# A second half that takes key and query groups in turn, the contraction behind them with every denominator, and row and key sums on VectorE

## The chip, the cores and the metric

One core of a Trainium2 chip runs the kernel. The metric is the device time of one launch in microseconds (us). The kernel before has a median of 2421.54 us over three runs (2417.6 to 2421.97).

## What is computed

The reference, cut to what matters (S = 2048 tokens, D = 1024, 32 heads of 32, F = 3584, all float32):

```python
xn = _layernorm(x)                      # (x - mean) / sqrt(var + 1e-5)
q, k, v = split(xn @ wqkv)              # 32 heads
phi = lambda t: where(t > 0, t + 1, exp(t)) + 1e-6
kv  = einsum("bhsd,bhse->bhde", phi(k), v)
z   = einsum("bhsd->bhd", phi(k))
num = einsum("bhqd,bhde->bhqe", phi(q), kv)
den = einsum("bhqd,bhd->bhq", phi(q), z)[..., None] + 1e-6
s   = (num / den) @ wo
h   = silu(xn @ w1) * (xn @ w3)         # the GLU is fed with xn too
out = x + s * silu(h @ w2)
```

## The kernel before, in words

**Arithmetic.** Each float32 operand is split into a high and a low part (ScalarE casts, line L93; VectorE subtracts, L94), and each product is three matmuls (L101, L102, L103). A 2x2 blocked product is made with seven block products instead of eight (`gemm`), so every operand also needs sums of its blocks: T1, T2, T3, T4 of the weights (VectorE, L342), S1 to S4 of the normalised rows.

**A gemm.** It uses four PSUM banks in the order a, b, c, d, a, c, d. VectorE adds the bank b to u (L453), c to make c22 (L460), d onto c22 (L466), then c21 (L481) and c12 (L489). The second product into bank c may start only when the add of L460 has read it. Behind each product the gemm takes one step of the next weight group (`next(stages)`) and one slot of `catch_up`: it runs the first entry of the list `later`, and if that is empty one step of the first generator in `jobs`. A gemm has six slots. Engines run in program order, so what a slot puts on VectorE stands between the gemm's own adds.

**Two halves of 1024 tokens** (`half(h)`): four key gemms (a pair of 128-column blocks each), four query gemms, then fourteen pairs of a gate and an up gemm. In the second half the key gemms are followed by the contraction (`row_products`): rows of x and of the keys are read back from DRAM and multiplied over all tokens, giving g_d, from which kv is made later (`key_values`, L902). Key gemms 0 and 1 of the second half run side by side.

**Keys.** phi is a relu (L495) and an exp (L496) on ScalarE and one VectorE operation (L497). The result pk is then turned by TensorE (`to_rows`, L503, into a bank trk) and copied by ScalarE (L504) to y; this turn is an entry of `later`. A fifth entry, `sums`, makes three sums on GpSimd (L538 to L540). GpSimd issues the stores to y_d (L507).

**Jobs in the slots.** In the first half: four `prepare_next` (normalise and turn 128-row blocks of the second half; four sums of row blocks on GpSimd, L259, L260, L267, L268), then 28 `weight_sums` of w2 (GpSimd, L755 to L758). In the second half: eight `denominators` jobs during the contraction (`first_denominators`); then, in the slots of the query and gate/up gemms, `key_values` and `merge_wo`, the divides of the first half's tokens, the other eight denominator jobs and eight more divides. A divide waits four slots when m < LATE, loads a tile qd through SyncE (L865) and works on VectorE (L873 and four sums). What is left of the jobs at the end of the half is run at once (`for j, _ in jobs: run(j)`). Tiles of jobs share four buffers (tag "job").

**GpSimd** also makes sums of the gated rows throughout (hs, L719 to L723), on 128x256 tiles. SyncE issues most loads in program order, so a load whose buffer is not free holds those behind it.

Of the kernel before, what the change touches and what calls it, by code (L numbers as in the profile page):

```python
# [16 lines left out]
P = 128  # L17
# [5 lines left out]
def tile_linear_attention_times_swiglu(  # L23
# [29 lines left out]

    ident = const.tile([P, P], F32, name="ident")
    make_identity(nc, ident)
    hmask = const.tile([P, P], F32, name="hmask")
    nc.vector.memset(hmask, 0.0)
    for i in range(P // DH):
# [55 lines left out]
    def small(name):  # L114
        return pc.tile([P, C], F32, tag="c", name=name)
# [105 lines left out]
    def prepare_next(i):  # L221


        def turn(n, src):
            p_ = bank(f"t{n}1_{i}")
            for k in range(ND // 2):
                nc.tensor.transpose(p_[:, k * P:(k + 1) * P], src[:, k * P:(k + 1) * P], ident)
            return p_

        def steps(_):  # L230
            t = [job_tile([P, D], f"xn{i}_{e}") for e in range(2)]
            for c in range(2):
# [24 lines left out]
            keep_rows(1, i, "A22", a22)  # L257
            g = job_tile([P, 2, C], f"xg{i}")
            nc.gpsimd.tensor_add(out=g[:, 0], in0=a21, in1=a22)  # L259
            nc.gpsimd.tensor_sub(out=g[:, 1], in0=a11, in1=a21)  # L260
# [6 lines left out]
            nc.gpsimd.tensor_sub(out=g[:, 0], in0=g[:, 0], in1=a11)  # L267
            nc.gpsimd.tensor_sub(out=g[:, 1], in0=a12, in1=g[:, 0])  # L268
            yield True
            keep_rows(1, i, "S2", g.rearrange("p n c -> p (n c)"))  # L270
            p_ = turn("A11", a11)
            keep("A11", p_)
            nc.scalar.copy(out=a11, in_=p_)
            yield True
            p_ = turn("A12", a12)
            keep("A12", p_)
            nc.scalar.copy(out=a12, in_=p_)
            yield True
            p_ = turn("A22", a22)
# [216 lines left out]
        nc.scalar.activation(dst, dst, AF.Exp, scale=-1.0)  # L496
        nc.vector.scalar_tensor_tensor(dst, src, 0.0, dst, op0=ALU.max, op1=ALU.add, accum_out=z)  # L497

    def to_rows(dst, src, name, bias=0.0):

        p_ = bank(f"tr{name}")
        for t in range(C // P):
            nc.tensor.transpose(p_[:, t * P:(t + 1) * P], src[:, t * P:(t + 1) * P], ident)  # L503
        nc.scalar.activation(dst, p_.rearrange("p (t d) -> p t d", t=C // P), AF.Identity, bias=bias)  # L504

    def keep_keys(h, pair, n, t):
        nc.gpsimd.dma_start(out=y_d[h][:, :, YS.index(n), pair], in_=t.rearrange("p (t d) -> p t d", d=P))  # L507

    def key_rows(h, pair):

        rows, pairs = {}, {}

        def use(n, c, src):
            j = 2 * pair + n
# [5 lines left out]
            later.append(lambda: turn(n, c, pk))  # L520

        def turn(n, c, pk):
            if (c, n) == (0, 0):
                t = rows[c, n] = small(f"y00_{h}_{pair}")
            else:
                if (1 - c, 1) not in pairs:
                    pairs[1 - c, 1] = job_tile([P, 2, C], f"y{c}_{h}_{pair}")
                t = rows[c, n] = pairs[1 - c, 1][:, n if c else 0]
            to_rows(t.rearrange("p (t d) -> p t d", d=P), pk, f"k{h}_{pair}_{n}{c}", 1e-6)
            if (c, n) != (1, 1):  # L530
                keep_keys(h, pair, f"Y{c}{n}", t)
            if len(rows) == 4:
                later.append(sums)

        def sums():
            y01, y10, y11 = rows[0, 1], rows[1, 0], rows[1, 1]
            r4, r2 = pairs[1, 1][:, 1], small(f"r2_{h}_{pair}")
            nc.gpsimd.tensor_add(out=r4, in0=y01, in1=y11)  # L538
            nc.gpsimd.tensor_sub(out=y11, in0=y11, in1=y10)
            nc.gpsimd.tensor_add(out=r2, in0=y11, in1=y01)  # L540
            for n, t in (("R4", r4), ("R5", y11), ("R2", r2)):
                keep_keys(h, pair, n, t)

        return use

    def row_products():
# [39 lines left out]
        for at, s in enumerate(steps):  # L586
# [3 lines left out]
            if at + 1 < len(steps):  # L590
                split_[steps[at + 1]] = ready(*steps[at + 1])
            if at + 2 == len(steps):
                ops["q1_0_"].ask()
# [49 lines left out]
    def half(h):  # L643
# [9 lines left out]
        def side_by_side(*gemms):  # L653
            for _ in zip_longest(*gemms):
                pass

        uses = [key_rows(h, pair) for pair in range(ND // 2)]
        if h == 0:
            mom = st.tile([P, TH, 2], F32, tag="mom", bufs=1, name="mom")
# [21 lines left out]
        if h == 0:  # L681
            for g in m:
                run(g)
        else:
            side_by_side(keys(0, paired=True), keys(1, paired=True))
            for pair in range(2, ND // 2):
                run(keys(pair))
            jobs.append((first_denominators(), False))
            for _ in row_products():
                pass  # L690
        jobs.append((attention_work(), False) if h else (next_work(), True))
        for pair in range(ND // 2):

            def use_q(n, c, src):
                j = 2 * pair + n
                pq = signed(f"pq{h}_{j}_{c}")
                phi(src, pq)
                nc.gpsimd.dma_start(out=pq_d[j // JG][2 * h + c][:, j % JG], in_=pq)  # L698
# [126 lines left out]
    def denominators(c):  # L825
# [29 lines left out]
    def divide(m, k):  # L855
# [12 lines left out]
            return t  # L868

        def steps(t):  # L870
            for _ in range(4 if m < LATE else 3):
                yield True
            nc.vector.scalar_tensor_tensor(t[:, :2], t[:, :2], 1e-6, t[:, 2:], op0=ALU.add, op1=ALU.mult)  # L873
            for _ in four_sums(t[:, 0], t[:, 1], t[:, 2], t[:, 3], nc.vector):
# [11 lines left out]
    def key_values(j):  # L886
# [87 lines left out]
    for h in range(NH):  # L974
        some = [Operands(wqkv, part * D + pair * 2 * P, f"{'qk'[part]}{h}_{pair}_", h == 0 and part == 1,
                         h and part == 1 and pair == 1)
                for part in (1, 0) for pair in range(ND // 2)]
# [6 lines left out]
    for o, o.next in zip(ops, ops[1:]):  # L984
        pass
    ops = {o.name: o for o in ops}
    after_rows = [ops["q1_0_"] in g for g in groups].index(True)
    ops["k1_3_"].next = None
    stages = in_turn(groups[:after_rows])
    for h in range(NH):  # L990
        half(h)
# [301 lines left out]
```

## Time and profile before

| what | value |
|---|---|
| median of three runs | 2421.54 us (2417.6 to 2421.97) |
| profiled execution, its own time | 2428.7 us |
| its span | 2426.6 us |
| TensorE (PE) matmul busy | 2325.3 us, 96% |
| VectorE (DVE) | 1802.1 us, 74% |
| ScalarE (ACT) | 921.9 us, 38% |
| GpSimd (POOL) | 748.2 us, 31% |
| granted TensorE clock, mean | 0.985 |

The span is what the trace covers; the profiled execution took 2.1 us more than its span. Times in the trace count from the start of the span. A row of the waits says which instruction stood still, for whom, how long in total, how often, and the longest of them. A row of the timeline has the start, the duration, the engine, the line, the operation, and in brackets the idle time before it and what ended it. PEclk is the share of the full TensorE clock that was granted.

### The profile page before, as it was taken

Reading aid. Unit: us, or ns where it says so; the run is one execution under the profiler, and the core shown is the slowest. Engines: PE = TensorE matmul, PEld = TensorE weight load, DVE = VectorE, ACT = ScalarE, POOL = GpSimd, SP = SyncE. Lnnn points to the kernel's source line nnn. Section 1 sums busy time; section 2 is a strip of 40 time slices with the busy share of each in tenths; the row PEclk is TensorE's granted clock in tenths of the full one; section 3 lists DMA queues with packets and bytes.
Section 4 is the critical chain, followed back from the end, with each engine's and each line's share of the span. In section 5 each row is a group of like instructions: output and inputs, shape, how many; then the busy total and the mean of one; then the engine's idle time right before and its main releaser. Section 6 shows DMA issues by size and latency. Waiting matters only on the chain.

```text
span 2426.6 us, 30936 instructions
## 1 busy us (share of the span) xinstructions
PE 2325.3 (96%) x10368; PEld 1903.0 (78%) x10368; DVE 1802.1 (74%) x2781; ACT 921.9 (38%) x1639; POOL 748.2 (31%) x892
## 2 busy tenths in 40 slices
PE   6899999899999989999999999998999999999997
PEld 5788778788888777878888888876777788888876
DVE  8888888878877746667777878777764676767698
ACT  5555333333332444445333333233322643343442
POOL 5331443558675320111242434323321000000033
PEclk9999999999999999999999999999999999999999
DMA  6455545566668567655555554556875665766688
GB/s 234 157 169 173 171 158 184 177 196 217 211 216 304 180 212 252 224 185 176 161 175 173 177 162 155 167 172 207 260 237 177 196 207 157 242 192 188 188 269 251
DMA packets 354015, 479.69 MB, mean 198 GB/s; under 512 B 24144, under 2 KB 262736, under 8 KB 353744
## 3 DMA queue, kind: packets, MB, share of 16 engines
q1 hardware_dynamic: 316608, 359.20, 46.9%
q0 software_dynamic: 37248, 118.52, 14.6%
q8 instruction: 81, 1.33, 0.2%
q14 instruction: 78, 0.64, 0.1%
HBM read 308.81 MB, written 172.49 MB: 198 GB/s over the span
## 4 chain that ended last, share of the span: by engine, by line
PE 70%; DVE 11%; DMA 8%; issue 6%; ACT 2%; POOL 1%; SPq 0%; POOLq 0%; DVEq 0%; ACTq 0%
PE g L101 1%; PE g L103 1%; PE g L102 1%; PE cB L101 1%; PE aB L101 1%; PE cB L102 1%; PE cB L103 1%; PE aB L102 1%; PE dB L101 1%; PE aB L103 1%; PE dB L102 1%; PE dB L103 1%; DMA qd<-pq_d 1%; DMA rA22B<-h_d 1%; DVE sg L736 1%
## 5 line engine op out<-in xcount | busy, mean ns | idle before, releaser
L740 POOL DMA_DIRECT2D h_d<-sg x112 | 83.0, 741 | 303.3 <-DVE sg L736 201.3
L1060 POOL DMA_DIRECT2D u_d<-uB x32 | 17.3, 542 | 407.8 <-DVE uB L1043 383.9
L94 DVE TENSOR_TENSOR xy<-xy,xy 128x512 fp32r<-128x512 f32 x112 | 81.1, 759 | 68.2 <-ACT xy L93 68.0
L93 ACT CAST xy<-xy 128x512 fp32r<-128x512 f32 x112 | 65.5, 621 | 103.7 <-PE g L103 65.8
L102 PE MATMUL g<-xy,xy 128*128 128x512 f32 x224 | 88.7, 396 | 0.0
L103 PE MATMUL g<-xy,xy 128*128 128x512 f32 x224 | 88.6, 396 | 0.0
L101 PE MATMUL g<-xy,xy 128*128 128x512 f32 x224 | 79.9, 401 | 2.9 <-ACT gu L625 2.7
L877 POOL DMA_DIRECT2D qs_d<-qd x32 | 17.9, 560 | 159.4 <-DVE qd L873 134.0
L507 POOL DMA_DIRECT2D y_d<-y x40 | 29.4, 742 | 118.1 <-ACT y L504 118.1
L1043 DVE TENSOR_TENSOR acc<-cB,acc 128x512 f32<-128x512 f32 x50 | 34.4, 688 | 41.0 <-PE cB L103 41.0
L1043 DVE TENSOR_TENSOR acc<-dB,acc 128x512 f32<-128x512 f32 x56 | 38.6, 689 | 30.9 <-PE dB L103 30.7
L722 POOL TENSOR_TENSOR hs<-sg 128x256 f32<-128x256 f32 x56 | 57.6, 1029 | 0.0
L720 POOL TENSOR_TENSOR hs<-hs,sg 128x256 f32<-128x256 f32 x56 | 56.4, 1011 | 0.1
L101 PEld LDWEIGHTS g<-xy,xy 128*128 128x128 f32 x224 | 42.5, 191 | 15.3 <-ACT gu L625 3.1
L723 POOL TENSOR_TENSOR hs<-sg,hs 128x256 f32<-128x256 f32 x56 | 52.5, 937 | 1.5
L698 POOL DMA_DIRECT2D pq_d<-pq x32 | 17.6, 549 | 111.7 <-DVE pq L497 103.0
L719 POOL TENSOR_TENSOR hs<-sg,sg 128x256 f32<-128x256 f32 x56 | 51.4, 917 | 1.2
L102 PEld LDWEIGHTS g<-xy,xy 128*128 128x128 f32 x224 | 42.9, 191 | 9.3 <-issue 0.4
L103 PEld LDWEIGHTS g<-xy,xy 128*128 128x128 f32 x224 | 42.8, 191 | 9.2
L755 POOL TENSOR_TENSOR w<-w 128x256 f32<-128x256 f32 x28 | 27.6, 987 | 66.0 <-DMA w<-in_B_w 54.5
L748 POOL DMA_DIRECT2D h_d<-hs x60 | 46.0, 768 | 3.0 <-POOL hs L723 1.8
L1174 POOL DMA_DIRECT2D s_d<-s x32 | 17.5, 546 | 85.6 <-DVE s L1043 56.9
(5311 smaller groups left out, 8427.1 us busy)
## 6 DMA issues: line engine op xcount, KB each, us to landing
h_d<-hs POOLq DMA_DIRECT2D x60, 256.0 KB, 3.6
h_d<-sg POOLq DMA_DIRECT2D x56, 256.0 KB, 5.2
w<-in_B_w SPq DMA_DIRECT2D x56, 256.0 KB
wt_d<-w SPq DMA_DIRECT2D x28, 512.0 KB
xy<-x_d SPq DMA_DIRECT2D x28, 512.0 KB
xy<-y_d SPq DMA_DIRECT2D x28, 512.0 KB
h_d<-hs SPq DMA_DIRECT2D x52, 256.0 KB
qs_d<-qd POOLq DMA_DIRECT2D x32, 384.0 KB, 4.0
```

What stands on the lines that cost most here:

```text
L93: nc.scalar.copy(out=hi, in_=src)
L94: return nc.vector.tensor_sub(out=lo, in0=src, in1=hi.bitcast(F32))
L101: nc.tensor.matmul(acc, lhsT=wh, rhs=ah, start=start, stop=False, skip_group_check=True)
L102: nc.tensor.matmul(acc, lhsT=wh, rhs=al, start=False, stop=False, skip_group_check=True)
L103: return nc.tensor.matmul(acc, lhsT=wl, rhs=ah, start=False, stop=stop, skip_group_check=True)
L719: e.tensor_add(out=s1, in0=a21, in1=a22)
L720: e.tensor_sub(out=s2, in0=s1, in1=a11)
L722: e.tensor_sub(out=s3, in0=a11, in1=a21)
L723: e.tensor_sub(out=s4, in0=a12, in1=s2)
L740: nc.gpsimd.dma_start(out=h_d[i][2 * h + c][:, 2 * n:4 * n + 2, k], in_=src)
L748: queue.dma_start(out=h_d[i][2 * h + c][:, 6 + 4 * e:10 + 4 * e, k], in_=o[e].rearrange("p (e s) -> p e s", s=P))
L1043: return V.tensor_add(out=c, in0=src, in1=c)
```

## The change

- **Order of the second half.** Keys 0 and queries 0 run side by side, then keys 1, queries 1, keys 2, queries 2, keys 3, queries 3. The contraction stands behind them, and the gate/up gemms follow it directly. The weight groups are ordered to match.
- **Denominators.** All sixteen denominator jobs run in the slots of the contraction, each one slot longer than before. `attention_work` has none any more; `key_values` has one slot less each, and a divide waits three slots in all cases.
- **Row sums.** The four sums of `prepare_next` go from GpSimd to VectorE, with one more slot between the two of each pair.
- **Key sums.** The entry `sums` of `later` is gone. Two of its three sums are made by VectorE in the turn of the last piece, one in the turn before it, and one operand of each is read from the PSUM bank of the turn. This holds for both halves. The bias 1e-6 comes from a tile `eps`.

The diff, cut to its core:

```diff
+    eps = const.tile([P, 1], F32, name="tiny")
+    nc.vector.memset(eps, 1e-6)
...
-            nc.gpsimd.tensor_add(out=g[:, 0], in0=a21, in1=a22)
-            nc.gpsimd.tensor_sub(out=g[:, 1], in0=a11, in1=a21)
+            nc.vector.tensor_add(out=g[:, 0], in0=a21, in1=a22)
+            yield True
+            nc.vector.tensor_sub(out=g[:, 1], in0=a11, in1=a21)
...
-            nc.gpsimd.tensor_sub(out=g[:, 0], in0=g[:, 0], in1=a11)
-            nc.gpsimd.tensor_sub(out=g[:, 1], in0=a12, in1=g[:, 0])
+            nc.vector.tensor_sub(out=g[:, 0], in0=g[:, 0], in1=a11)
+            yield True
+            nc.vector.tensor_sub(out=g[:, 1], in0=a12, in1=g[:, 0])
...
         def turn(n, c, pk):
+            V = nc.vector
+            p_ = turned(pk, f"k{h}_{pair}_{n}{c}")
             if (c, n) == (0, 0):
+                y00 = small(f"y00_{h}_{pair}")
+                nc.scalar.activation(y00, p_, AF.Identity, bias=eps)
+                keep_keys(h, pair, "Y00", y00)
+            elif (c, n) == (1, 1):
+                rows["y01"] = job_tile([P, 2, C], f"y01_{h}_{pair}")
+                nc.scalar.copy(out=rows["y01"][:, 1], in_=p_)
+            elif (c, n) == (1, 0):
...
+                nc.scalar.activation(y10, p_, AF.Identity, bias=eps)
+                V.tensor_sub(out=r5, in0=rows["y01"][:, 1], in1=p_)
...
             else:
...
+                nc.scalar.activation(y01, p_, AF.Identity, bias=eps)
+                V.scalar_tensor_tensor(r4, p_, 2e-6, r4, op0=ALU.add, op1=ALU.add)
+                V.scalar_tensor_tensor(r2, p_, 1e-6, r5, op0=ALU.add, op1=ALU.add)
...
-        def sums():
-            y01, y10, y11 = rows[0, 1], rows[1, 0], rows[1, 1]
-            r4, r2 = pairs[1, 1][:, 1], small(f"r2_{h}_{pair}")
-            nc.gpsimd.tensor_add(out=r4, in0=y01, in1=y11)
-            nc.gpsimd.tensor_sub(out=y11, in0=y11, in1=y10)
-            nc.gpsimd.tensor_add(out=r2, in0=y11, in1=y01)
...
-            side_by_side(keys(0, paired=True), keys(1, paired=True))
-            for pair in range(2, ND // 2):
+            side_by_side(keys(0, paired=True), queries(0, paired=True))
+            for pair in range(1, ND // 2):
                 run(keys(pair))
-            jobs.append((first_denominators(), False))
+                run(queries(pair))
+            jobs.append((all_denominators(), False))
             for _ in row_products():
                 pass
         jobs.append((attention_work(), False) if h else (next_work(), True))
-        for pair in range(ND // 2):
...
-            run(gemm(ops[f"q{h}_{pair}_"], A, use_q))
+        if h == 0:
+            for pair in range(ND // 2):
+                run(queries(pair))
...
         def steps(e, half, t):
             yield True
+            yield True
             if not den:
...
-            for _ in range(4 if m < LATE else 3):
+            for _ in range(3):
                 yield True
...
         def steps(e, t):
-            yield True
             if not acc:
...
-    def first_denominators():
+    def all_denominators():
         yield from spread_z()
-        yield from go_on([j for c in H0 for j in denominators(c)])
+        yield from go_on([j for c in range(NCH) for j in denominators(c)])
...
-        work += [j for c in H1 for j in denominators(c)]
```

How the order of instructions moves is shown at three places. Numbers behind a tile's name tell its copies apart, and lines of the changed kernel lie 2 to 12 higher (L460 becomes L464, L342 becomes L346, L94 becomes L96, L503 becomes L507, L873 becomes L885).

VectorE before, in the fourth gate gemm of the first half (wu is the raw up weight, T3u and T2u its split sums, c22g the gate's c22):

```order
L736 TENSOR_TENSOR sg_2_10_2773<-c12u_2__2931,sg_2_10_2773 128x512
L342 TENSOR_TENSOR wu_3__2775<-wu_3__2775 128x4x128 x2
L94 TENSOR_TENSOR T3u_3__2965<-wu_3__2775,T3u_3__2965 128x512
L453 TENSOR_TENSOR ug_3__2948<-bg_3__2973,ug_3__2948 128x512
L342 TENSOR_TENSOR wu_3__2775<-wu_3__2775 128x4x128
L94 TENSOR_TENSOR T2u_3__2990<-wu_3__2775,T2u_3__2990 128x512
L342 TENSOR_TENSOR wu_3__2775<-wu_3__2775 128x4x128
L460 TENSOR_TENSOR c22g_3__3012<-cg_3__2974,ug_3__2948 128x512
L94 TENSOR_TENSOR T1u_3__3014<-wu_3__2775,T1u_3__3014 128x512
```

And the same place in the change (xg holds two of the row sums):

```order
L747 TENSOR_TENSOR sg_2_10_2779<-c12u_2__2936,sg_2_10_2779 128x512
L346 TENSOR_TENSOR wu_3__2781<-wu_3__2781 128x4x128 x2
L96 TENSOR_TENSOR T3u_3__2970<-wu_3__2781,T3u_3__2970 128x512
L457 TENSOR_TENSOR ug_3__2953<-bg_3__2974,ug_3__2953 128x512
L261 TENSOR_TENSOR xg_2996<-xn_1_2761 128x512
L346 TENSOR_TENSOR wu_3__2781<-wu_3__2781 128x4x128
L464 TENSOR_TENSOR c22g_3__3010<-cg_3__2975,ug_3__2953 128x512
L263 TENSOR_TENSOR xg_2996<-xn_0_2760,xn_1_2761 128x512
L96 TENSOR_TENSOR T2u_3__2991<-wu_3__2781,T2u_3__2991 128x512
```

A row sum has come in ahead of the c22 add, and the split of T2u with one sum has gone behind it.

TensorE before, where the keys of pair 2 of the second half are turned (the digits behind trk are the pair and the piece; dk, ak and bk are products of the gemms):

```order
L503 MATMUL trk_2_11_6921<-ident,pk_5_1_6882 128x128 x4
L101 MATMUL dk_2__6819<-S_1_6420,B22k_2__6763 128x512
...
L503 MATMUL trk_2_00_6951<-ident,pk_4_0_6910 128x128 x4
L101 MATMUL ak_3__6979<-A_1_6414,B11k_3__6786 128x512
...
L503 MATMUL trk_2_01_6993<-ident,pk_4_1_6941 128x128 x4
L101 MATMUL bk_3__7000<-S_1_6415,T2k_3__6834 128x512
```

TensorE in the change, where the keys of pair 1 are turned; pairs 2 and 3 read the same there, and pair 3 of before read so too:

```order
L507 MATMUL trk_1_11_6866<-ident,pk_3_1_6857 128x128 x4
L103 MATMUL dk_1__6809<-S_1_6426,B22k_1__6748 128x512
...
L507 MATMUL trk_1_00_6895<-ident,pk_2_0_6885 128x128 x4
L507 MATMUL trk_1_01_6926<-ident,pk_2_1_6917 128x128 x4
L103 MATMUL aq_1__6963<-A_1_6420,B11q_1__6772 128x512
```

The third turn no longer has the twelve matmuls of the next gemm's first product between itself and the second one.

VectorE before, in the last gate gemm of the second half (qd are the tiles of divides):

```order
L94 TENSOR_TENSOR T3u_13__13450<-wu_13__13263,T3u_13__13450 128x512
L342 TENSOR_TENSOR wu_13__13263<-wu_13__13263 128x4x128
L873 SCALAR_TENSOR_TENSOR qd_2_13535<-qd_2_13535 128x512
L453 TENSOR_TENSOR ug_13__13330<-bg_13__13348,ug_13__13330 128x512
L719 TENSOR_TENSOR qd_2_13535<-qd_2_13535 128x128
L722 TENSOR_TENSOR qd_2_13535<-qd_2_13535 128x128
L94 TENSOR_TENSOR T2u_13__13470<-wu_13__13263,T2u_13__13470 128x512
L720 TENSOR_TENSOR qd_2_13535<-qd_2_13535 128x128
L460 TENSOR_TENSOR c22g_13__13379<-cg_13__13349,ug_13__13330 128x512
```

And in the change:

```order
L96 TENSOR_TENSOR T3u_13__13505<-wu_13__13335,T3u_13__13505 128x512
L346 TENSOR_TENSOR wu_13__13335<-wu_13__13335 128x4x128
L457 TENSOR_TENSOR ug_13__13397<-bg_13__13415,ug_13__13397 128x512
L96 TENSOR_TENSOR T2u_13__13525<-wu_13__13335,T2u_13__13525 128x512
L346 TENSOR_TENSOR wu_13__13335<-wu_13__13335 128x4x128
L464 TENSOR_TENSOR c22g_13__13446<-cg_13__13416,ug_13__13397 128x512
```

No divide stands there any more; the last one of these stands between the c22 adds of the gate and the up gemm of the pair before.

More of the change, by code (lines that the diff above doesn't have):

```diff
@@ L497, in phi, with turned @@
         nc.vector.scalar_tensor_tensor(dst, src, 0.0, dst, op0=ALU.max, op1=ALU.add, accum_out=z)
-    def to_rows(dst, src, name, bias=0.0):
+    def turned(src, name):
         p_ = bank(f"tr{name}")
@@ L503, in to_rows @@
             nc.tensor.transpose(p_[:, t * P:(t + 1) * P], src[:, t * P:(t + 1) * P], ident)
[L504 removed]
+        return p_
     def keep_keys(h, pair, n, t):
@@ L509, in key_rows @@
     def key_rows(h, pair):
-        rows, pairs = {}, {}
+        rows = {}
         def use(n, c, src):
@@ L522, in turn @@
         def turn(n, c, pk):
+            V = nc.vector
+            p_ = turned(pk, f"k{h}_{pair}_{n}{c}")
             if (c, n) == (0, 0):
-                t = rows[c, n] = small(f"y00_{h}_{pair}")
-            else:
[L526 to L533, printed above, removed]
-        def sums():
-            y01, y10, y11 = rows[0, 1], rows[1, 0], rows[1, 1]
-            r4, r2 = pairs[1, 1][:, 1], small(f"r2_{h}_{pair}")
-            nc.gpsimd.tensor_add(out=r4, in0=y01, in1=y11)
-            nc.gpsimd.tensor_sub(out=y11, in0=y11, in1=y10)
-            nc.gpsimd.tensor_add(out=r2, in0=y11, in1=y01)
-            for n, t in (("R4", r4), ("R5", y11), ("R2", r2)):
-                keep_keys(h, pair, n, t)
+                y00 = small(f"y00_{h}_{pair}")
[5 more added lines that the diff above has]
+            elif (c, n) == (1, 0):
+                y10, r5 = (rows.setdefault("y10", job_tile([P, 2, C], f"y10_{h}_{pair}"))[:, e] for e in range(2))
+                nc.scalar.activation(y10, p_, AF.Identity, bias=eps)
+                V.tensor_sub(out=r5, in0=rows["y01"][:, 1], in1=p_)
+                keep_keys(h, pair, "Y10", y10)
+                keep_keys(h, pair, "R5", r5)
+            else:
+                (y01, r4), r5, r2 = (rows["y01"][:, e] for e in range(2)), rows["y10"][:, 1], small(f"r2_{h}_{pair}")
+                nc.scalar.activation(y01, p_, AF.Identity, bias=eps)
+                V.scalar_tensor_tensor(r4, p_, 2e-6, r4, op0=ALU.add, op1=ALU.add)
+                V.scalar_tensor_tensor(r2, p_, 1e-6, r5, op0=ALU.add, op1=ALU.add)
+                for n_, t in (("Y01", y01), ("R4", r4), ("R2", r2)):
+                    keep_keys(h, pair, n_, t)
         return use
@@ L592, in row_products @@
             if at + 2 == len(steps):
-                ops["q1_0_"].ask()
+                ops["g1_0_"].ask()
                 stages = in_turn(groups[after_rows:])
@@ L655, in side_by_side, with queries, use_q @@
                 pass
+        def queries(pair, **how):
+            def use_q(n, c, src):
+                j = 2 * pair + n
+                pq = signed(f"pq{h}_{j}_{c}")
+                phi(src, pq)
+                nc.gpsimd.dma_start(out=pq_d[j // JG][2 * h + c][:, j % JG], in_=pq)
+            return gemm(ops[f"q{h}_{pair}_"], A, use_q, **how)
         uses = [key_rows(h, pair) for pair in range(ND // 2)]
@@ L691, in half @@
         jobs.append((attention_work(), False) if h else (next_work(), True))
-        for pair in range(ND // 2):
[L694 to L698, printed above, removed]
-            run(gemm(ops[f"q{h}_{pair}_"], A, use_q))
+        if h == 0:
+            for pair in range(ND // 2):
+                run(queries(pair))
         for pair in range(NF // 2):
@@ L974, in tile_linear_attention_times_swiglu @@
     for h in range(NH):
+        order = [(part, pair) for part in (1, 0) for pair in range(ND // 2)]
+        if h:
+            order = [(part, pair) for pair in range(ND // 2) for part in (1, 0)]
         some = [Operands(wqkv, part * D + pair * 2 * P, f"{'qk'[part]}{h}_{pair}_", h == 0 and part == 1,
-                         h and part == 1 and pair == 1)
-                for part in (1, 0) for pair in range(ND // 2)]
+                         h and part == 0 and pair == 0)
+                for part, pair in order]
         some += [Operands((w1, w3)[e], pair * 2 * P, f"{'gu'[e]}{h}_{pair}_", second=h == 0 and e and pair == NF // 2 - 1)
@@ L986, in tile_linear_attention_times_swiglu @@
     ops = {o.name: o for o in ops}
-    after_rows = [ops["q1_0_"] in g for g in groups].index(True)
-    ops["k1_3_"].next = None
+    after_rows = [ops["g1_0_"] in g for g in groups].index(True)
+    ops["q1_3_"].next = None
     stages = in_turn(groups[:after_rows])
```

## The prediction

> **What bounds the kernel now.** I read the page first. TensorE is the bound, so only what makes it stand still or run slowly can move the time.
>
> ```profile
> span 2426.6 us, 30936 instructions
> ...
> PE 2325.3 (96%) x10368; PEld 1903.0 (78%) x10368; DVE 1802.1 (74%) x2781; ACT 921.9 (38%) x1639; POOL 748.2 (31%) x892
> ```
>
> The change adds and removes no matmul; it moves them. So the sum is made from TensorE's waits. First, over the whole span, those that the change touches:
>
> ```profile
> PE trk L503 <- DVE pk L497: 10.9, 3, 5.7
> PE cg__13349 L101 <- DVE c22g__13379 L460: 9.6, 1, 9.6
> PE kv L902 <- DMA gw<-g_d: 5.1, 1, 5.1
> ...
> PE g L101 <- ACT gu L625: 2.7, 1, 2.7
> PE cs L101 <- DVE s L1050: 2.4, 1, 2.4
> ```
>
> Then the waits between 200 and 500 us, in the first half's gate gemms 1 to 6, while `prepare_next` and `weight_sums` fill the slots. All six are the same wait, the second product into bank c behind the c22 add:
>
> ```profile
> PE cg__3948 L101 <- DVE c22g__3982 L460: 4.1, 1, 4.1
> PE cg__2328 L101 <- DVE c22g__2366 L460: 3.8, 1, 3.8
> PE cg__2974 L101 <- DVE c22g__3012 L460: 3.8, 1, 3.8
> PE cg__3620 L101 <- DVE c22g__3658 L460: 3.7, 1, 3.7
> PE cg__2656 L101 <- DVE c22g__2690 L460: 1.7, 1, 1.7
> PE cg__3302 L101 <- DVE c22g__3336 L460: 1.5, 1, 1.5
> ```
>
> A wait costs more than itself. The windows of 12 us that begin where these waits end show it in the column behind PE's busy time, the granted clock (266, 352, 483: gate gemms 1, 3 and 6; 825 and 874: key turns; 904: gu; 1678: the 9.6; 1743: the 2.4):
>
> ```profile
> 266.00:278.00 12.00, 11.17 (x46) 0.86 0.48 145
> 352.00:364.00 12.00, 11.45 (x48) 0.86 0.49 150
> 483.00:495.00 12.00, 11.78 (x40) 0.75 0.53 154
> 825.00:837.00 12.00, 11.10 (x47) 0.78 0.47 155
> 874.00:886.00 12.00, 11.85 (x49) 0.86 0.78 261
> 904.00:916.00 12.00, 11.96 (x54) 0.86 0.54 187
> 1678.00:1690.00 12.00, 11.83 (x41) 0.77 0.77 241
> 1743.00:1755.00 12.00, 11.97 (x53) 1.00 0.79 236
> ```
>
> 0.86 over 12 us is 0.14 x 12 = 1.7 us lost, 0.78 is 2.6, 0.77 is 2.8, 0.75 is 3.0. So waits of 2.7 us and more lose 1.7 to 3.0 us besides; the wait of 2.4 us loses nothing. The threshold lies between 2.4 and 2.7 us. [...]
>
> **First half's gates.** Now: stalls 4.1 + 3.8 + 3.8 + 3.7 + 1.7 + 1.5 = 18.6 us, clock 1.7 + 1.7 + 3.0 and, for gate 5 as for its likes 1 and 3, 1.7: 8.1 us, together 26.7 us. VectorE's own row just ahead of the late c22 add in gate gemm 1:
>
> ```profile
> 262.34 2.17 DVE L94 TENSOR_TENSOR T2u__2344<-wu__2129,T2u__2344 128x512 fp32r<-128x512 f32 x1 [0.75 <-ACT T2u__2344 L93]
> 264.54 1.63 DVE L342 TENSOR_TENSOR wu__2129<-wu__2129 128x512 f32<-128x512 f32 x1
> 266.10 0.68 DVE L460 TENSOR_TENSOR c22g__2366<-cg__2328,ug__2302 128x512 f32<-128x512 f32 x1
> ```
>
> ```profile
> 263.90 1.73 POOL L267 TENSOR_TENSOR xg<-xg,xn 128x512 f32<-128x512 f32 x1
> ```
>
> L342 ends half a microsecond behind GpSimd's row sum; it took 1.63 us, where the c22 add, which has an operand in PSUM, took 0.68. The same at 334 us, ahead of gate gemm 3:
>
> ```profile
> 334.55 3.46 DVE L736 TENSOR_TENSOR sg<-c21u__2903,sg 128x512 f32<-128x512 f32 x1
> ```
>
> ```profile
> 334.91 1.30 POOL L259 TENSOR_TENSOR xg<-xn 128x512 f32<-128x512 f32 x1
> 336.17 1.29 POOL L260 TENSOR_TENSOR xg<-xn,xn 128x512 f32<-128x512 f32 x1
> ```
>
> Two row sums on GpSimd cost VectorE 3.46 - 0.68 = 2.8 us; made by VectorE itself I price them at 0.68 each, 1.4 us (between 0.68 and this 3.46). With this and the order of instructions:
> - Gate 1: the pair ahead gains 2.8 - 1.4 = 1.4 us, L342 gains 1.63 - 0.68 = 0.95: 3.8 becomes some 1.4; T2u should gain too, so 1.0.
> - Gates 3 and 5: T2u's split (and its wait of 0.75 for ScalarE) goes behind the c22 add, worth 2.17 + 0.75 + 0.95 = 3.9 us by the rows of gate 1; one row operation comes in ahead, 0.7 to 0.9. With the pair's 1.4 as well: 0 and 0.3.
> - Gates 2 and 4: no GpSimd row sum stands there; one more VectorE operation does: 1.7 + 0.7 = 2.4 and 1.5 + 0.7 = 2.2. That is just under the threshold.
> - Gate 6: `weight_sums` now begin later and no longer run beside it, so it should look like gates 2 and 4: 2.3.
>
> That is 8.2 us, and one loss of 1.7 for a wait that passes the threshold: 9.9. Term: 9.9 - 26.7 = **-16.8** (ends: 0 if VectorE gains nothing; -26.7).
>
> **First half's keys.** One of the three trk waits is here: 10.9 - 5.7 - 3.1 (the row at 874 below) = 2.1 us; it goes with GpSimd's key sums. But the turn 01 of pair 2 now stands right behind the turn 11. Before, these were their times:
>
> ```profile
> 115.57 0.66 PE L503 MATMUL trk<-ident,pk 128*128 128x128 f32 x4
> ```
>
> ```profile
> 118.97 0.69 DVE L497 SCALAR_TENSOR_TENSOR pk<-c21k__1125,pk 128x512 f32<-128x512 f32 x1
> ```
>
> At those times the second turn, ready to start at some 116.0, would wait until 119.66, 3.7 us, and at best not at all. VectorE loses GpSimd's company ahead of it, so I take the middle, 2.0, and 0.5 for pair 3, whose two operations stand closer together. Term: -2.1 + 2.5 = **+0.4** (-2 to +5).
>
> **Second half's key turns.** In pair 3 of before the turn 01 follows the turn 00 directly, and this is what comes of it:
>
> ```profile
> 871.71 0.62 ACT L495 ACTIVATE pk<-c21k__7109 128x512 f32<-128x512 f32 x1
> 872.23 0.62 ACT L495 ACTIVATE pk<-c12k__7136 128x512 f32<-128x512 f32 x1
> 872.75 1.14 ACT L496 ACTIVATE pk<-pk 128x512 f32<-128x512 f32 x2
> ```
>
> ```profile
> 874.15 0.66 PE L503 MATMUL trk<-ident,pk 128*128 128x128 f32 x4 [3.06 <-DVE pk L497]
> ```
>
> Behind the copy of the turn 00, ScalarE makes two relus and two exps, and only then VectorE can finish pk. The change has this order in pairs 1, 2 and 3; before, pair 2 had twelve matmuls in between and no wait. Two more of 3.06 + 1.7: **+9.5** (0 to +20). Pair 0 keeps its 5.7.
>
> **gu.** ScalarE stands in front of the copies of gu, in a cast whose rows have not come:
>
> ```profile
> 902.89 0.62 ACT L93 CAST xy<-xy 128x512 fp32r<-128x512 f32 x1 [4.40 <-DMA xy<-x_d]
> ```
>
> SyncE's queue is late because loads of denominators and of yy wait for buffers (860 to 945 us):
>
> ```profile
> SPq L558 <- PE den L840: 17.1, 4, 5.3
> SPq L831 <- PE den L840: 14.6, 3, 10.4
> ```
>
> In the change four denominator tiles are loaded ahead of the contraction and each job takes a slot more, so the first steps should find their rows: -(2.7 + 1.7) = **-4.4** (0 at worst). The yy tiles, which share those buffers, come later: **+0.5** (0 to +3).
>
> **kv.** It waits 5.1 us for g_d now. In the change twelve matmuls fewer stand ahead of it, 12 x 0.23 (the window at 1743: 53 matmuls in 12 us) = 2.7 us; about 1 us of VectorE operations fewer stand behind the contraction's end: **+1.8** (0 to +4).
>
> **Denser slots.** `merge_wo` and the divides now fill gates 0 to 12 more tightly, each divide with five VectorE operations; nothing of it waited before but by a few tenths: **+2** (0 to +8).
>
> **Last divides.** Before, the jobs left over stand in the last pair. In the trace between 1640 and 1680 us VectorE stands for their loads, ahead of the c22 add of gate 13:
>
> ```profile
> DVE qd L873 <- DMA qd<-pq_d: 11.5, 3, 5.0
> ```
>
> All of these are done by pair 12 in the change, since the slots of the query gemms' denominators are free and a divide takes a slot less. The 9.6 goes with its clock of 2.8: **-12.4** (0 at worst). What is late next there is the same add behind split operations, as in the gates from 7 on, none of which stands among the waits above.
>
> **Sum.** -16.8 + 0.4 + 9.5 - 4.4 + 0.5 + 1.8 + 2 - 12.4 = -19.4. The span 2426.6 becomes 2407.2. The profiled execution took 2428.7, 7.2 above the median of 2421.54, so against the median: 2421.5 - 19.4 = **2402 us**. I take 0.2%, 4.8 us, as what a measurement can tell from no change.
>
> **Rivals.**
> - *VectorE gains nothing in the first half.* GpSimd's hs sums remain, and VectorE has 40 operations more; then that term is 0: -2.6, **2419 us**. For it: gates 2 and 4 wait with no row sum beside them. Against it: the 3.46 us row.
> - *Row sums are held in their turn.* Each of them reads two SBUF operands like L342, which took 0.95 us more beside one GpSimd operation. With 1 us more each, gates 2, 4 and 6 wait some 3.3 us and lose 1.7 of clock: 3 x 2.7 = 8.1 more, **2410 us**. [...]
> - *The new key turns do not wait*, because ScalarE reaches the relus in time: -28.9, **2393 us**. Against it: the same order waited in pair 3.
> - *They wait like pair 0*, 5.7 + 2.6 (0.78 over 12 us) in three pairs, 24.9 instead of the 14.3 in the sum: +10.6, **2413 us**.
> - *The last divides do not do what they should*: the loads of qd come late in pair 12 just the same: +12.4, **2414 us**.
> - *Slower: the contraction is starved.* SyncE loads the remaining twelve denominator tiles in the same queue as the rows, and each that stands for a buffer holds the rows behind it, as at 902.89. A stall like gu costs 2.7 + 1.7 = 4.4. From six of them on the gain is gone (-19.4 + 26.4 = +7.0); with eight, **2437 us**. Against it: no other step of the contraction waited before, with eight tiles.
>
> **Chances.** Forecast 0.38; held row sums 0.12; turns without wait 0.13; turns like pair 0 0.08; late divides 0.07; no gain on VectorE 0.12; starved contraction 0.10. Faster by over 0.2% (under 2416.7): all but the last two, 0.78. Within 0.2%: 0.12. Slower: 0.10. The range reaches from the turns without wait, and a little beyond for the ends of the gates' term, to the case with no gain on VectorE: 2389 to 2421.
>
> **What would show it.** In the changed kernel: waits of cg behind L464 of 0 to 2.5 us in gates 1 to 6; no GpSimd row or key sums, and VectorE's operations there near 0.7 us; three to four waits of trk near 3 us between 800 and 900 us with the clock at 0.86 behind them; no wait on gu; kv waiting some 7 us; no wait at gate 13. The forecast is wrong if the gates of the first half still wait for 15 us or more, or if the contraction shows new waits on rows.

## The result and the profile after

The changed kernel takes **2391.91 us** (median of four runs, 2388.13 to 2395.18); the kernel before took 2419.74 us in the same comparison. The ratio is 0.9884, with a 95% interval of 0.9866 to 0.9903: faster by 28 us, where 19 were forecast. The forecast was 2402, the range 2389 to 2421.

One execution of a kernel differs from the next by several us: runs of the kernel before lay between 2411.4 and 2427.21 in the later comparisons, and its two profiled executions took 2428.7 and 2424.7. So medians stand for the time here, and profiles for the waits.

The page of the changed kernel:

```profile
span 2389.9 us, 30981 instructions
...
PE 2313.4 (97%) x10368; PEld 1895.4 (79%) x10368; DVE 1776.6 (74%) x2822; ACT 925.6 (39%) x1639; POOL 693.4 (29%) x852
```

VectorE has 41 instructions more and is 25.5 us less busy (1802.1 before): its other operations became shorter, as the 112 splits of xy, which took 759 ns on average before and take 704. TensorE's waits between 200 and 540 us, where six waits added up to 18.6 us before:

```profile
PE cg__3303 L103 <- DVE c22g__3335 L464: 1.3, 1, 1.3
PE cg__2661 L103 <- DVE c22g__2693 L464: 0.5, 1, 0.5
PE cg__4259 L103 <- DVE c22g__4292 L464: 0.3, 1, 0.3
```

And two rows of the waits of the whole span:

```profile
PE trk L507 <- DVE pk L501: 16.9, 6, 5.7
...
PE kv L913 <- DMA gw<-g_d: 2.8, 1, 2.8
```

Four of the six waits of trk stand in the second half (780 to 960 us):

```profile
PE trk L507 <- DVE pk L501: 15.2, 4, 5.7
```

The waits on gu and at gate 13 are gone. The windows of 12 us behind the four waits of the key turns (at 800, 827, 873 and 918 us), behind kv (1117) and behind the longest wait on cs (4.4 us, 1714; the longest before was 2.4); the clock is the column behind PE's busy time:

```profile
800.00:812.00 12.00, 11.70 (x45) 0.77 0.70 235
827.00:839.00 12.00, 11.97 (x45) 0.76 0.35 102
873.00:885.00 12.00, 12.00 (x50) 0.86 0.38 111
918.00:930.00 12.00, 12.00 (x51) 0.86 0.71 215
1117.00:1129.00 12.00, 11.65 (x59) 1.00 0.92 269
1714.00:1726.00 12.00, 12.00 (x47) 0.88 0.85 277
```

The key turns lose 2.8, 2.9, 1.7 and 1.7 us of clock besides their waits.

### The profile page after: what moved, and what is told of

Read it like the earlier page. It is cut to its first block, busy times and chain, and to the rows that moved or that the text cites. A ratio compares the mean times of both kernels' runs of the same rounds, so it can differ in the third digit from the quotient of the medians.

```text
span 2389.9 us, 30981 instructions
## 1 busy us (share of the span) xinstructions
PE 2313.4 (97%) x10368; PEld 1895.4 (79%) x10368; DVE 1776.6 (74%) x2822; ACT 925.6 (39%) x1639; POOL 693.4 (29%) x852
## 4 chain that ended last, share of the span: by engine, by line
PE 42%; issue 9%; DMA 7%; DVE 5%; POOL 3%; ACT 1%; SPq 0%; POOLq 0%; DVEq 0%; ACTq 0%
PE g L103 2%; PE g L104 2%; PE g L105 2%; PE cB L103 1%; PE cB L104 1%; PE dB L104 1%; PE dB L103 1%; PE dB L105 1%; PE cB L105 1%; PE aB L103 1%; PE aB L104 1%; PE aB L105 1%; POOL h_d L751 1%; DMA xy<-y_d 1%; DMA qs_d<-qd 1%
## 5 line engine op out<-in xcount | busy, mean ns | idle before, releaser
L96 DVE TENSOR_TENSOR xy<-xy,xy 128x512 fp32r<-128x512 f32 x112 | 74.8, 704 | 67.5 <-ACT xy L95 67.5
L103 PEld LDWEIGHTS g<-xy,xy 128*128 128x128 f32 x224 | 41.6, 188 | 15.2 <-issue 4.5
```

Source lines behind the costliest of these rows:

```text
L96: return nc.vector.tensor_sub(out=lo, in0=src, in1=hi.bitcast(F32))
L103: nc.tensor.matmul(acc, lhsT=wh, rhs=ah, start=start, stop=False, skip_group_check=True)
```

## Experiments

### The row sums back on GpSimd, in the same slots

```diff
-            nc.vector.tensor_add(out=g[:, 0], in0=a21, in1=a22)
+            nc.gpsimd.tensor_add(out=g[:, 0], in0=a21, in1=a22)
             yield True
-            nc.vector.tensor_sub(out=g[:, 1], in0=a11, in1=a21)
+            nc.gpsimd.tensor_sub(out=g[:, 1], in0=a11, in1=a21)
```

The second pair of sums is edited in the same way.

> The changed kernel with the sixteen row sums back on GpSimd, in the slots where the change has them; key sums and order of the second half as changed. Theory H (VectorE was held by GpSimd's row sums): the waits of cg in gate gemms 1 to 6, now 2 us together, come back to 8 to 14 us with clock, so 2400 to 2408 us. Rival P (what counted was the new place of the row sums and weight splits among the slots): the waits stay under 4 us, 2391 to 2395 us.

Measured: 2405.3 us, ratio to the kernel before 0.9946 (0.9924 to 0.9967), against 0.9884 of the changed kernel; the intervals do not meet. The waits between 200 and 540 us:

```profile
PE cg__2334 L103 <- DVE c22g__2372 L464: 4.0, 1, 4.0
PE cg__2975 L103 <- DVE c22g__3010 L464: 3.3, 1, 3.3
PE dg__3620 L103 <- DVE c22g__3651 L470: 2.4, 1, 2.4
```

9.7 us of waits instead of 2.1, and the clock in the 12 us behind them is 0.75, 0.87 and 0.86, another 6.2 us, where the changed kernel has 1.00. This is how it comes to the first of them, gate 1, on VectorE and then on GpSimd:

```profile
252.24 6.57 DVE L346 TENSOR_TENSOR wu__2135<-wu__2135 128x512 f32<-128x512 f32 x2
```

```profile
255.60 1.42 POOL L731 TENSOR_TENSOR hs<-hs,sg 128x256 f32<-128x256 f32 x2
256.98 1.28 POOL L270 TENSOR_TENSOR xg<-xg,xn 128x512 f32<-128x512 f32 x1
```

The two weight sums of this row end after 6.57 us, at 258.81, just behind GpSimd's hs sums and its row sum (258.26). In the changed kernel the same two take 2.12 (at 250.32) and 0.68 us (at 252.96), and the split, the sum and the c22 add of gate 1 are these:

```profile
257.43 0.70 DVE L96 TENSOR_TENSOR T2u__2350<-wu__2135,T2u__2350 128x512 fp32r<-128x512 f32 x1 [0.75 <-ACT T2u__2350 L95]
258.16 1.10 DVE L346 TENSOR_TENSOR wu__2135<-wu__2135 128x512 f32<-128x512 f32 x1
259.19 0.68 DVE L464 TENSOR_TENSOR c22g__2372<-cg__2334,ug__2312 128x512 f32<-128x512 f32 x1
```

Before, these three took 2.17, 1.63 and 0.68 us. Theory H holds: with their slots unchanged, the engine of the row sums is worth some 13 us by the times (2405.3 - 2391.9) and 15 by the two ratios; the profiles give 7.6 us of waits and 6.2 of clock.

### The added slots taken away, the row sums on VectorE

```diff
             nc.vector.tensor_add(out=g[:, 0], in0=a21, in1=a22)
-            yield True
             nc.vector.tensor_sub(out=g[:, 1], in0=a11, in1=a21)
```

The second pair of sums is edited in the same way.

> The changed kernel without the two added slots of prepare_next; the row sums stay on VectorE, two in a row. Theory H: VectorE is not held, so 2390 to 2396 us, with cg waits of gates 1 to 6 under 5 us. Rival P: the waits return to 8 us and more with clock, 2400 us and above.

Measured: 2397.04 us, 0.9913 (0.9886 to 0.9941). The waits of the gates:

```profile
PE cg__3961 L103 <- DVE c22g__4000 L462: 3.0, 1, 3.0
PE cg__2669 L103 <- DVE c22g__2705 L462: 1.4, 1, 1.4
PE cg__3315 L103 <- DVE c22g__3351 L462: 1.2, 1, 1.2
```

5.6 us of waits, a little over what H allowed and well under what P asked for; the time lies between the two, nearer H, and its interval still meets that of the changed kernel. That the slots have a part of their own is not shown: there are 3.5 us more of waits than in the changed kernel, but 3.0 us stand at gate 6 (cg__3961), and with the first half of the kernel before the wait there moves by as much from execution to execution (see its second profile).

### The row sums and their slots alone, on the kernel before

The edit is the one to `prepare_next` in the diff of the change, and nothing else.

> The kernel before with the row sums on VectorE and the two added slots, and nothing else of the change. The first half's gates then account for the most of the gain by themselves: cg waits of gates 1 to 6 fall from 18.6 us to 2 to 8, and the time to 2394 to 2402 us. If the gain needs the rest of the change: above 2408 us.

Measured: 2403.36 us, 0.9941 (0.9922 to 0.996). There is no wait of a gate between 200 and 540 us at all. But at the change of halves a new one stands, on a split sum of the first key weights:

```profile
PE bk__6485 L103 <- DVE T2k__6334 L94: 3.7, 1, 3.7
PE bk__6485 L101 <- ACT T2k__6334 L93: 3.6, 1, 3.6
```

So a part of what the gates gave was given back 200 us later, 7.3 us, of which the key turns behind it make good 3.0 (5.7 us of waits instead of 8.7). The time just misses the expected 2394 to 2402. In the changed kernel this wait is 0.6 and 1.2 us; why it is not as long there was not tried.

### The key sums alone

The edit is `turned`, `key_rows` and `eps` of the diff on the kernel before.

> The kernel before with the key sums on VectorE, reading PSUM, and nothing else of the change. If the key sums only move the turns: the wait of 2.1 us at 100 us goes, and pair 2 of the second half gets the wait of pair 3 (3.1 and 1.7 of clock), so 2419 to 2424 us. If GpSimd's relief pays on the key gemms: 2414 to 2418 us.

Measured: 2416.35 us against 2417.27, ratio 0.9993 (0.998 to 1.0007): no difference that can be told. The time lies in the second band of the expectation, but the kernel before ran as fast in this comparison, so neither case is borne out by it. The turns did what was expected, three waits in the second half where there were two (8.7 us before):

```profile
PE trk L505 <- DVE pk L499: 12.3, 3, 5.8
```

Not expected was the first half, where nothing of `prepare_next` was edited:

```profile
PE cg__3961 L103 <- DVE c22g__4000 L462: 4.4, 1, 4.4
PE cg__2669 L103 <- DVE c22g__2705 L462: 3.2, 1, 3.2
PE cg__3315 L103 <- DVE c22g__3351 L462: 2.6, 1, 2.6
```

With two more of 0.4 and 0.2 us that is 10.8 us instead of 18.6, and other gates. The fifth entry of `later` is gone, so the steps of `prepare_next` fall into other slots of the gemms. The profile shows 8 us less of waits here and the median 1 us; 3.6 us go back at the key turns, and the rest is not settled: the profiled execution, of 2412.88 us, was the shortest of this kernel's runs. The wait on gu is gone in this run too, although no denominator was moved.

### The order and the denominators, with the sums left on GpSimd

The edit is all of the diff but `prepare_next`, `turned`, `key_rows` and `eps`.

> The kernel before with the new order of the second half and the new denominators; row sums and key sums stay on GpSimd. By the sum of the prediction: key turns +9.5, gu -4.4, last divides -12.4, small terms +4.3, so -3: 2413 to 2418 us. If the order is worth more than that: 2408 us or less.

Measured: 2407.92 us, 0.9957 (0.994 to 0.9973), against 2420.86 of the kernel before in the same comparison: 10 to 13 us, where the sum had given 3. Some 4 us of the difference are kv, which I had put at +1.8 us and which waits 2.8 us here as well, 2.3 less than before, with about the same loss of clock behind it (0.86). The rest was not taken apart. Part of it may not be the edit's: gate 6 waits 0.9 us here instead of 4.1, in a first half that this run does not touch.

### The order alone, with the denominators of before

Against the run before it:

```diff
-            yield True
             yield True
             if not den:
...
-            for _ in range(3):
+            for _ in range(4 if m < LATE else 3):
...
         def steps(e, t):
+            yield True
             if not acc:
...
-        yield from go_on([j for c in range(NCH) for j in denominators(c)])
+        yield from go_on([j for c in H0 for j in denominators(c)])
...
+        work += [j for c in H1 for j in denominators(c)]
```

> As the run before it, but with the denominators, slots and divides of the kernel before. The four query gemms no longer offer slots to the attention work, so if the denominators' move pays for the order, more divides are left over at the end of the half: the wait at gate 13 or behind it grows, and the time is 2425 us or more. If the order needs no such help: within 4 us of the run before it.

Measured: 2448.61 us, 1.0118 (1.0103 to 1.0133): slower by 28 us. The waits between 1600 and 1800 us:

```profile
PE B11s L101 <- ACT XA11s L93: 46.7, 1, 46.7
```

The query gemms no longer carry attention work, so the half ends with jobs left over, and they run while TensorE stands. The new order by itself loses. What pays for it in the run before is the denominators' move together with the fewer slots of the divides and of `key_values`; these were not tried one by one with the new order.

### Slots: one more per divide on the changed kernel, one less on the kernel before

On the changed kernel:

```diff
-            for _ in range(3):
+            for _ in range(4 if m < LATE else 3):
                 yield True
```

> The changed kernel with four waiting slots per divide for m < LATE again, all else as changed. If the count of slots decides (24 slots more are asked for, some eight more than there are): two divides are left over, stand in or behind gate 13, and a few us are lost, 2393 to 2402 us. If only the place of the denominators counts: 2390 to 2394 us and no new wait at gate 13.

Measured: 2400.86 us, 0.9908 (0.9886 to 0.993). By the medians that is 9 us slower than the changed kernel; the intervals of the two ratios still meet. Two divides are left for pair 13, and VectorE stands for loads of divides, so products of two up gemms wait that did not in the changed kernel. TensorE over the whole span, and VectorE between 1600 and 1720 us:

```profile
PE du__13218 L103 <- DVE c22u__13252 L470: 2.9, 1, 2.9
PE cu__11974 L103 <- DVE c22u__12004 L464: 2.8, 1, 2.8
```

```profile
DVE qd L885 <- DMA qd<-pq_d: 9.0, 2, 5.7
```

On the kernel before:

```diff
-            for _ in range(4 if m < LATE else 3):
+            for _ in range(3):
                 yield True
...
         def steps(e, t):
-            yield True
             if not acc:
```

> The kernel before with one slot less per divide and per key_values job, and nothing else of the change: order, denominators, row and key sums as before. If the last divides are repaired by slots alone: the wait of 8 to 10 us at gate 13 and its clock go, 2405 to 2411 us. If they need the denominators in the contraction: the wait stays, 2416 us or more.

Measured: 2404.68 us, 0.9928 (0.9904 to 0.9951): 16 us for two lines, 0.3 us below the expected band. The wait at gate 13 and its clock make 12.4 of them. The longest wait that is left between 1600 and 1800 us is this, where cs waited 2.4 us before; no gate waits more than 0.4:

```profile
PE cs L101 <- DVE s L1049: 5.6, 2, 5.4
```

The jobs of the second half ask for a number of slots, and what is asked for beyond those that there are is paid at the end. The kernel before has 32 gemms with six slots, 192, and asked for some 208 by a count of the yields: 16 too many, and 9.6 us of wait. With the order alone there are 168 for the same 208, 40 too many, and 46.7 us of wait. The changed kernel asks for 152 of 168; of the 56 saved, 40 are the slots of the divides and of `key_values` and 16 the denominators that moved. With one slot more for each of 24 divides it is 176, eight too many, and the two waits of 2.9 and 2.8 us above. Neither the order nor the place of the denominators is needed to repair gate 13.

The same run tells of kv. Its row there:

```profile
PE kv L901 <- DMA gw<-g_d: 3.0, 1, 3.0
```

The wait is 3.0 us without the order, the denominators or the sums, where it was 5.1. Up to that point the run differs from the kernel before in the slot of `key_values` only. SyncE's queue shows what goes with that slot. In the kernel before, GpSimd issues the last store of g_d at 1047.62 us, and ahead of the load that waits for this store SyncE issues the load of a whole weight block:

```profile
1048.56 0.37 SPq L322 DMA_DIRECT2D wq__8562<-in_A_wqkv  x1
1051.07 1.20 SPq L892 DMA_DIRECT2D gw<-g_d  x2
```

kv starts at 1056.05, 8.4 us behind the store. In all five profiles with the slot (two of the kernel before, the row sums alone, the key sums alone, the order alone) a weight load stands at this place and the way from the store to kv takes 7.9 to 8.6 us. In the seven without the slot none stands there, and it takes 5.7 to 5.9 us. That the weight load is what makes the way longer is likely, but no run moved it by itself.

### The key turns put later

On the changed kernel, an empty entry ahead of the third turn of a pair (two for pair 0), and turns that may not be issued ahead of the products of their slot; the two were not tried one by one:

```diff
         if later:
-            later.pop(0)()
+            with ExitStack() as behind:
+                for m in marks:
+                    behind.enter_context(tc.issue_after(m.ins))
+                later.pop(0)()
...
+            if h and (n, c) == (0, 1):
+                later.extend([lambda: None] * (1 if pair else 2))
             later.append(lambda: turn(n, c, pk))
```

> The changed kernel with the third key turn of the second half's pairs put behind a product of the next gemm (two products for pair 0). If the waits of 5.7, 3.2, 3.2 and 3.2 us and the clock behind them come from the turn standing too early: all go, -15.2 of wait and -10 of clock, 2366 to 2376 us. If ScalarE or VectorE is only late by the same in another place: waits of another row take over, 2385 us or more.

Measured: **2374.5 us**, ratio to the kernel before 0.9813 (0.9799 to 0.9828), 17 us under the changed kernel and faster than both. The turns between 780 and 1100 us, and the windows behind the places where the first two waits had stood:

```profile
PE trk L510 <- DVE pk L504: 1.7, 3, 0.9
PE ak__6765 L103 <- ACT uk__6764 L444: 1.6, 1, 1.6
```

```profile
799.00:811.00 12.00, 11.86 (x56) 1.00 0.56 185
821.00:833.00 12.00, 11.67 (x56) 1.00 0.46 141
1098.00:1110.00 12.00, 11.81 (x53) 0.86 0.90 266
```

15.2 us of waits became 3.3 us with ak, and the clock stays at 1.00. All four waits came from the turn standing too early in TensorE's order.

### The kernel before, profiled a second time

> The kernel before once more, for a second profile. If the waits of its gates are a property of the program: the six cg waits again together 17 to 20 us, with the wait of 9 to 10 us at gate 13. If the first profile was an odd execution: sums that differ by 5 us or more.

It took 2424.7 us. The first two and the late one of its waits:

```profile
PE cg__3948 L101 <- DVE c22g__3982 L460: 4.0, 1, 4.0
PE cg__2328 L101 <- DVE c22g__2366 L460: 3.8, 1, 3.8
```

```profile
PE cg__13349 L101 <- DVE c22g__13379 L460: 7.9, 1, 7.9
```

The six gate waits add up to 18.6 us once more (4.0 + 3.8 + 3.7 + 3.7 + 1.8 + 1.6): they are no accident of the first profile. Gate 6 is not the program's alone, though. Up to 1043 us the run with fewer slots gives every engine the same work in the same order as the kernel before, and there gate 6 has

```profile
PE cg__3948 L101 <- DVE c22g__3982 L460: 0.6, 1, 0.6
```

with 1.00 in the 12 us behind it. The run with the order and the denominators has 0.9. The other five gates stay within 0.2 us in all these profiles. Ahead of gate 6's c22 add, VectorE's split of xo (the normalised rows of `prepare_next`) took 3.02 us in the first profile and 0.68 us with fewer slots. The late wait, behind loads, moves by 1.7 us between the two profiles of the kernel before.

## Why the prediction was right, term by term

| term | forecast, us | the two profiles, us |
|---|---|---|
| first half's gates | -16.8 | waits 18.6 to 2.1, clock 8.1 to 0: -24.6 |
| first half's keys | +0.4 | trk 2.1 to 1.7: -0.4 |
| second half's key turns | +9.5 | trk 8.7 to 15.2, clock 4.3 to 9.1: +11.3 |
| gu | -4.4 | gone: -4.4 |
| kv | +1.8 | 5.1 to 2.8, clock 1.4 to 0: -3.7 |
| last divides | -12.4 | gone: -12.4 |

The six add up to -34.2 us, of 36.7 between the two spans. Behind the gates, between 1700 and 1780 us, two waits moved that no term had: as (4.7 us before, with 0.75 over the 12 us behind it) is gone, and cs rose from 2.4 to 6.9 us, with 0.88 behind the longest, together some -1.8. The medians are 28 apart, since the profiled execution of before was longer than its median. For the two small terms, yy and denser slots, the profile shows no wait above 0.7 us in the contraction and at the gates behind it; they were not taken apart. Gates and kv gained more than forecast and only the key turns lost more, so the time lies 10 us under the forecast and 3 us inside the range.

- **First half's gates: mechanism right, size too small.** The term that was mis-sized is the rest of 9.9 us that I left, above all 2.4, 2.2 and 2.3 for gates 2, 4 and 6; 0.5, 1.3 and 0 were measured. I added one operation of 0.7 us to gates that had waited 1.5 to 1.7 us and gave them no relief, since no row sum of GpSimd stood beside them. But VectorE came to them less late; which operation ahead of gates 2 and 4 made the difference was not taken apart. Gate 6 is in part luck: its 4.1 us and the 3.0 us of clock behind it are 7.1 of the 24.6, and with the first half of before it waited only 0.6 and 0.9 us in two other runs. The row sums themselves were priced rightly at 0.68; the trace of the changed kernel has, for the first two of each block, minimum, median and maximum in ns:

```profile
L261 DVE TENSOR_TENSOR xg<-xn x4: 676/678/887, 163.2 to 423.1; 128x512 f32<-128x512 f32 x4
...
L263 DVE TENSOR_TENSOR xg<-xn,xn x4: 676/680/682, 163.8 to 423.7; 128x512 f32<-128x512 f32 x4
```

- **Key turns: right.** The row of pair 3 of before gave the price for pairs 1, 2 and 3 of the change. ScalarE's rows ahead of the third turn, in pair 2 of the changed kernel, and what TensorE did:

```profile
870.52 0.62 ACT L499 ACTIVATE pk<-c21k__7247 128x512 f32<-128x512 f32 x1
871.04 0.62 ACT L499 ACTIVATE pk<-c12k__7281 128x512 f32<-128x512 f32 x1
871.56 1.14 ACT L500 ACTIVATE pk<-pk 128x512 f32<-128x512 f32 x2
```

```profile
872.97 0.66 PE L507 MATMUL trk<-ident,pk 128*128 128x128 f32 x4 [3.16 <-DVE pk L501]
```

  The wait is 3.16 where 3.06 was read. The rival of turns without a wait fell with it, and so did that of waits like pair 0's.
- **Last divides: right in size, and the reason named was only half of it.** I named both the denominators' slots and the slot less per divide; the run on the kernel before shows that fewer slots alone suffice.
- **gu: right in size, the reason not shown.** I named the denominator tiles loaded ahead of the contraction. The wait is also gone with the key sums alone and with the order alone, where the denominators are those of before, so this is not the only way to it.
- **kv: wrong in sign.** The step that failed is "twelve matmuls fewer stand ahead of it". Fewer did stand there, 24 instead of 36 behind the contraction, and kv still waited less: its data came sooner, 5.7 us behind the last store of g_d instead of 8.4. The clock behind it had been

```profile
1056.00:1068.00 12.00, 11.95 (x55) 0.88 0.58 180
```

  before, and was 1.00 after. The run with fewer slots puts the shorter wait on the slot of `key_values`; by which step the slot lengthens the way, the weight load ahead of it or another, stays open. The 1.4 us of clock are luck: in the seven profiles without the slot kv waits 2.7 to 3.0 us, and the clock behind it fell in four of them, to between 0.75 and 0.86, and stayed at 1.00 in three (the last section shows for two traces on what it depended).
- **Rivals.** "VectorE gains nothing" and "row sums are held" fell: the gates lost their waits, and the sums ran at 0.68. "The contraction is starved" fell: no wait above 0.7 us on its rows. What the rival of held row sums started from was measured again: with GpSimd's row sums back, the two weight sums at gate 1 took 6.57 us beside GpSimd's sums, where the changed kernel has 2.12 and 0.68. VectorE's row sums could have gone the same way, but of the eight above only one took longer than 0.69 us, and that one 0.89; the other eight took 0.68 to 0.69. That two operands in SBUF are what makes an operation longer, as that rival had it, was not shown.

## What to carry to other kernels

Where one engine's work beside another's lengthens what the bound waits for, move the cause, and price the receiver by its own undisturbed rows: sixteen operations of 0.68 us on the busier engine were cheaper than the same on the idle one (2391.9 us against 2405.3). Count the slots that background jobs ask for against the slots that there are; the excess comes due near the end of the loop, here in the worst case in one piece of 46.7 us. And read in the order of instructions what stands directly behind what: here two instructions side by side that share a chain on another engine cost 3.2 us and then 1.7 to 2.9 us of clock.

## What the hardware showed that I had not expected

The prediction put a threshold between 2.4 and 2.7 us, above which a wait costs the clock. The length alone does not settle it. kv waited 2.8 us in the changed kernel and the window behind it has 1.00; with the key turns put later it waited 2.7 us and the window at 1098 has 0.86, as behind the 2.7 of gu before. With the row sums back on GpSimd, a wait of 2.4 us has 0.86 behind it (436 us); cs's 2.4 us of before has 1.00.

The record of the clock in the traces of the kernel before and of the changed kernel shows what went with it. The clock recorded there is either full or half (1.00 or 0.50). The stretches at half clock last 3.41, 6.83 or 10.24 us, one, two or three times 3.41, but for the one at the very end of each trace (11.44 and 9.52 us). Within a trace they all begin on one grid of 3.41 us; it begins 0.87 us behind the start of the span in the one and 3.34 us in the other. Count, from 90 us on, how long TensorE stood in each cell of that grid that ran at full clock: in the two traces together the cell behind it ran at half clock in all 17 cases of 1.95 us or more, and in none of some 1300 below 1.5; of the six between, the one of 1.94 us was followed by half clock and the five of 1.52 to 1.63 were not. These are the cells of gu's 2.7 us and of cs's 2.4 us before, each with the one that follows:

```profile
898.57:901.98 3.41, 2.78 (x12) 1.00 0.94 277
901.98:905.40 3.42, 1.35 (x6) 1.00 1.07 382
905.40:908.81 3.41, 3.41 (x10) 0.50 0.47 174
1738.24:1741.65 3.41, 2.38 (x11) 1.00 0.94 312
1741.65:1745.07 3.42, 2.04 (x9) 1.00 0.66 228
1745.07:1748.48 3.41, 3.41 (x17) 1.00 0.88 239
```

Of gu's wait 2.1 us lay in one cell; cs's was cut by the grid into 1.0 and 1.4 us, and kv's 2.8 in the changed kernel into 1.5 and 1.3. The 2.4 us of the run with the row sums back on GpSimd lay nearly whole in one stretch of 3.4 us, with half clock behind it:

```profile
432.80:436.20 3.40, 1.18 (x8) 1.00 0.40 129
436.30:439.60 3.30, 3.23 (x8) 0.50 0.37 153
```

So, as an estimate from these counts, a single wait of between 1.6 and some 4 us costs the clock in this kernel or not by where the grid happens to cut it. One cell at half clock costs up to 0.5 x 3.41 = 1.7 us.
